# Three small reorderings in a TensorE-bound kernel: the attention's dense matmuls, V's job and the tail's products

## The chip, the cores and the metric

The kernel runs on one core of a Trainium2 chip. The metric is the device time of one execution in microseconds; the medians are over several executions. Every run named here is fast: the granted TensorE clock is 1.00 in all of them. Because the effects are of some tenths of a microsecond in 650, most of the argument is read from traces: each trace is one execution and has the start of its instructions (in four traces 52 matmul records are missing, see below), and the same wait in two traces agrees to about 0.01 us where nothing acts on it.

## The reference

The layer normalises x, computes attention in four segments of 512 tokens with a memory of the earlier segments, adds a token-mixing MLP, and adds x. The change touches the attention's second half only:

```python
for s in range(4):                                   # segments; 32 heads of 32
    logits = q_s k_s^T * scale + mask                # a causal mask
    a_dot  = softmax(logits) v_s
    a_mem  = phi(q_s) M / (phi(q_s) z + 1e-6)        # memory of earlier segments
    o      = g * a_mem + (1 - g) * a_dot             # g: a gate per head
    M, z   = M + phi(k_s)^T v_s, z + sum phi(k_s)
out = x + concat(o) @ wo + MLP(xn)                   # xn: x normalised
```

## The kernel before

The attention runs in 32 units, one for each segment and group of four heads. In a unit TensorE (PE) computes logits in two or three bursts, ScalarE (ACT) takes their exponentials (1.88 us each), GpSimd (POOL) masks the diagonal blocks of pT, and PE weighs the values in three parts for the unit before. Between these, PE runs *dense* jobs of eight 512-column matmuls: the projections q, k and V, and the output product ("wo"). How many dense matmuls stand between two steps is set by `cuts`. An even unit from 18 on reads: logits 0, `cuts[1]` dense matmuls, weighing part 0, `cuts[2]`, part 1, `cuts[3]`, part 2, logits 1, `cuts[5]`, logits 2, the rest.

```python
def unit_jobs(self, u):
    jobs = [self.wo_job(*self.wo_jobs.popleft())] if 10 <= u < self.QUOTA_FROM else []   # QUOTA_FROM is 18
    m = u // 4 + 1
    if m < 2 * N_SEG:
        jobs.append(self.v_job(m, u % 4))
    ...                                              # then q of unit u + 2, and k up to unit 15
# in attention()
    if u >= 18 and even:
        cuts = self.cut(total, (0, 4, 1, 4, 0, 9, 6))
```

Each job takes the next of two banks of PSUM (the memory that the matmuls of this kernel write their results to) in turn, so a job waits until the job *two before it* has been copied out of its bank. Who copies differs: q and (from unit 8) V are copied by ACT, k and wo by VectorE (DVE). wo's copy is an addition to `fin` of some 0.69 us.

```python
# q_job: ACT copies        # k_job: DVE copies        # v_job: ACT (for m > 2)        # wo_job: DVE adds to fin
def dense(self, n, side=True):
    while n > 0 and self.jobs:
        job = self.jobs[0]
        ...
        if b is None:
            b = job[1] = 6 + self.turn               # banks 6 and 7 in turn
            self.turn ^= 1
        ...                                          # matmuls up to the next stop
        if stop == 8:
            end(b)                                   # the copy, or the addition to fin
            self.jobs.popleft()
        elif self.side and stop in stops:
            self.side.popleft()()                    # one step of DVE's side work
```

Side work is DVE's part of the unit before and of the next: the scales, `pqT` (phi of q), `prod` (the weighed sums times their scales, 1.22 us), `o_s` (their addition), phi of k, and at times a normalisation (`xs`). DVE also fetches the weighed sums themselves ("the sums", `ost`, from banks 4 and 5; parts 0 and 2 of the weighing share bank 4). DVE carries these out in the order in which the program emits them.

The tail, after unit 31, multiplies the last segment's eight groups of oT (`o_s` transposed) with wo. Group 6 of oT comes by a DMA that transposes o_s of unit 30; group 7 by PE itself:

```python
...
product(3, 0, 6)                 # product n over groups 0 to 5
for n in range(3):
    product(n, 6, 7)             # the seventh group's part of products 0, 1, 2
product(4, 0, 7)
self.o_transpose(u, 4)
...
```

Of the kernel before, what the change touches and what calls it, by code (L numbers as in the profile page):

```python
# [386 lines left out]
class _Kernel:  # L387
# [1111 lines left out]
    def unit_jobs(self, u):  # L1499
        jobs = [self.wo_job(*self.wo_jobs.popleft())] if 10 <= u < self.QUOTA_FROM else []  # L1500
        m = u // 4 + 1
        if m < 2 * N_SEG:
            jobs.append(self.v_job(m, u % 4))
        if u + 2 < N_UNIT:
            jobs.append(self.q_job(u + 2))
            if u + 2 < N_UNIT // 2:
                jobs.append(self.k_job(u + 2))
            else:
                self.k_load(u + 2)
        if u >= self.QUOTA_FROM:  # L1510
            quota = self.QUOTA[u % 2] if u + 1 < N_UNIT else 100
            quota -= 8 * len(jobs) + sum(8 - j[0] for j in self.jobs)
            while quota > 0 and self.wo_jobs:
                jobs.append(self.wo_job(*self.wo_jobs.popleft()))
                quota -= 8
            self.left = max(-quota, 0)
        return jobs
# [5 lines left out]
    def attention(self):  # L1523
        self.jobs, self.turn, self.left = deque(), 0, 0
        self.side, self.stops = deque(), self.STOPS
        self.exps, self.in_etmp = [], [None] * 4
        self.wo_jobs = deque((c, half) for c in range(4 * (N_SEG - 1)) for half in range(2))
        self.jobs.extend([self.q_job(0), self.k_job(0)] + [self.v_job(0, c) for c in range(4)])
        self.dense(16)
        self.late_exps()  # L1530
        self.phi_k(0)
        self.k_transpose(0)
        self.jobs.extend([self.q_job(1), self.k_job(1)])
        self.dense(100)
        for u in range(N_UNIT):
            if u == N_GRP:
                t, R = _Walk(self.mem, self.B_AT + self.STG_AT, self.B_AT + self.S2_AT).take(
                    "oT2", [P, N_GRP, SEG_L], BF16, N_GRP)
                self.oT.append(t)
                self.R_oT.append(R)  # L1540
                self.load_fin(0)
                self.load_fin(1)
            if 1 <= u <= N_GRP:
                self.fw.dma(self.wo[:, u - 1, :], self.A_wo[(u - 1) * P:u * P, :], writes=[self.R_wo[u - 1]])
            even = u % 2 == 0
            self.jobs.extend(self.unit_jobs(u))
            total = 8 * len(self.jobs) - sum(j[0] for j in self.jobs) - self.left
            xn = self.XN_AT.index(u) + 4 if u in self.XN_AT else None
            if u in self.XN_AT[::4]:
                self.xn_load(xn)  # L1550
                self.xn_load(xn + 1)
            if u >= 18 and even:
                cuts = self.cut(total, (0, 4, 1, 4, 0, 9, 6))
            elif u < 10 or u >= 14 and total <= 26:
                cuts = self.cut(total, (0, 4, 2, 4, 1, 13, 8) if even else (7, 3, 2, 4, 1, 15))
            else:
                cuts = self.cut(total, (0, 4, 2, 2, 2, 14, 8) if even else (7, 3, 2, 2, 2, 16))
            end = u >= N_UNIT - 4
            self.stops = self.STOPS_FEW if total <= 26 and u >= 14 else self.STOPS
            self.dense(cuts[0])  # L1560
            self.logits(u, 0)
            self.dense(cuts[1], end)
            while end and self.side:
                self.side.popleft()()
            if u:
                self.weigh(u - 1, 0)
            self.dense(cuts[2], False)
            if u:
                self.weigh(u - 1, 1)
            self.dense(cuts[3], False)  # L1570
            if u:
                self.weigh(u - 1, 2)
                steps = self.combine(u - 1)
                last = steps[-1]
                steps[-1] = lambda u=u, last=last: (last(), self.o_transpose_dma(u - 1))
                self.side.append(steps.pop(0))
            if N_GRP <= u:
                self.side.append(lambda u=u: self.phi_q(u))
            if u:
                self.side.extend(steps)  # L1580
            if u + 1 < N_UNIT:
                self.side.append(lambda u=u: (self.phi_k(u + 1), self.k_transpose(u + 1)))
            if xn is not None:
                self.side.append(lambda c=xn: (self.xn_scale(c), self.xn_transpose(c), c % 4 < 2 and self.xn_load(c + 2)))
            self.dense(cuts[4])
            self.logits(u, 1)
            if even:
                self.dense(cuts[5])
                self.logits(u, 2)
            self.dense(8 * len(self.jobs) - sum(j[0] for j in self.jobs) - self.left)  # L1590
        while self.side:
            self.side.popleft()()
        self.tail()
# [10 lines left out]
    def tail(self):  # L1604
        fw = self.fw
        s, u = N_SEG - 1, N_UNIT - 1
        fin, R_fin = self.fin, self.R_fin
        for i in range(2, 4):
            self.load_fin(4 * s + i)
        fw.wait_outputs(3)  # L1610

        def product(n, j0, j1, cols=((0, 512),)):
            i, h, b = n // 2, n % 2, (6 + self.turn, 0, 1, 2, 3, 7 - self.turn, 5, 4)[n]
            for p, (c0, c1) in enumerate(cols):
                with fw.group(reads=self.R_wo[j0:j1] + self.R_oT[s % 3][j0:j1], writes=[self.R_bank[b]]):
                    for jc in range(j0, j1):
                        fw.mm(self.ps[:, b, c0:c1], self.oT[s % 3][:, jc, i * P:(i + 1) * P],
                              self.wo[:, jc, h * 512 + c0:h * 512 + c1], start=(jc == 0), stop=(jc == N_GRP - 1))
                if j1 < N_GRP:
                    return  # L1620
                dst = fin[i][:, h * 512 + c0:h * 512 + c1]
                R = Res("fin")
                R.w = R_fin[i][h].w
                fw.op("dve", lambda e: e.tensor_tensor(dst, self.ps[:, b, c0:c1], dst.bitcast(F16), op=ALU.add),
                      reads=[self.R_bank[b], R], writes=[R])
                fw.dma(self.out_d[:, 4 * s + i, h * 512 + c0:h * 512 + c1], dst, reads=[R],
                       is_output=True, issuer=("sp", "act")[p % 2])
                b = (b + 1) % 3

        product(0, 0, 6)  # L1630
        product(1, 0, 6)
        self.weigh(u, 0)
        self.weigh(u, 1)
        product(2, 0, 6)
        self.weigh(u, 2)
        for step in self.combine(u):
            step()
        product(3, 0, 6)
        for n in range(3):
            product(n, 6, 7)  # L1640
        product(4, 0, 7)
        self.o_transpose(u, 4)
        product(3, 6, 7)
        product(5, 0, 5)
        for n in range(5):
            product(n, 7, 8)
        product(5, 5, 8)
        product(6, 0, 8)
        product(7, 0, 8, ((0, 256), (256, 384), (384, 512)))
# [28 lines left out]
```

## Time and profile before

| what | value |
|---|---|
| median time | 653.07 us (652.82 to 653.62, 6 runs) |
| span of the profiled execution | 651.30 us |
| from its start to the first logits | 387.46 us |
| first to last logits ("attention") | 243.48 us |
| last logits to the last matmul ("tail") | 17.86 us |

Lines from the profile page of the kernel before: the span, the busy time of each engine with its share of the span, and the chain of work that ended last, by engine.

```profile
span 651.3 us, 11181 instructions
...
PE 645.6 (99%) x4611; PEld 303.2 (47%) x4611; DVE 433.7 (67%) x808; ACT 281.3 (43%) x305; POOL 153.0 (23%) x179
...
PE 94%; DVE 2%; DMA 1%; ACT 1%; POOL 1%; issue 0%; DVEq 0%
```

PE is busy 99% of the span and makes 94% of the chain. The change adds and removes no matmul, so it can win only PE's waits. The view of waits of the kernel before, for PE, has five lines (who waited for whom: us in total, times, longest). These two lie in the stretch that the change touches; two others (DVE's brow, 1.3 us, and h, 0.3) lie ahead of the attention, and one (ACT's pT, 0.2) is in unit 0:

```profile
PE ps_all L199 <- DMA oT<-o_s: 0.5, 1, 0.5
PE ps_all L199 <- POOL pT L1368: 0.4, 2, 0.2
```

These figures are too small, and a learner should see why. A 512-column matmul stands in the trace with 0.38 us, but the next one starts 0.216 us after it. The Trainium skill ("Perfetto Trace Analysis", "Tensor Engine Instruction") says that a TensorE instruction's end is estimated and not observed. A wait shorter than the 0.16 us between these two figures is therefore invisible, and a longer one shows only its rest. So I read *starts*: for each matmul I took the start of the next, less 0.216 us after 512 columns, 0.056 after 132, 0.025 after 33; in front of a logits burst 0.096 us are regular, and behind one 0.09 to 0.10, and these are taken off too. What remains is called *excess*. The largest in the kernel before:

| where (unit) | excess, us | what PE waited for |
|---|---|---|
| tail | 0.70 | the DMA that transposes o_s of unit 30 |
| weighing, units 20, 22, 24 | 0.37, 0.22, 0.37 | POOL's mask |
| weighing, unit 16 | 0.25 | POOL's mask |
| V's job, unit 11 | 0.30 | DVE's copy of k out of the bank |
| V's job, units 22 and 26 | 0.16, 0.07 | ACT's copy of the job two before |
| logits 1, unit 0 | 0.22 | the exponentials before; the same in every run |
| logits 0, even units from 20 | 0.09 each | the exponentials before |

The following fences are from the timelines of the kernel before (start in us, length in us, engine, line, operation, output and inputs, forms, count; in brackets the engine's idle time and who ended it). First the tail:

```profile
635.64 2.03 SPq L221 DMA_TRANSPOSE oT<-o_s  x1
...
637.95 1.46 PE L199 MATMUL ps_all<-wo,oT 128*128 128x512 bf16 x6
...
639.94 2.33 PE L199 MATMUL ps_all<-wo,oT 128*128 128x512 bf16 x10 [0.53 <-DMA oT<-o_s]
...
642.11 0.39 PE L205 MATMUL ps_all<-ident,o_s 128*128 128x128 bf16 x4
```

The DMA is issued at 635.64. PE's six matmuls from 637.95 are through by 639.25 (6 times 0.216), but the next starts at 639.94: 0.70 us, of which the bracket shows 0.53. Next unit 20, where the fourth line is weighing part 0:

```profile
545.66 1.22 DVE L1465 TENSOR_TENSOR prod<-ost,srec 128x1024 bf16<-128x1024 bf16 x1
...
545.86 2.28 POOL L1368 TENSOR_SCALAR_AFFINE_SELECT pT<-pT 128x512 bf16<-128x512 bf16 x2 [2.78 <-ACT pT L1364]
...
546.27 1.04 PE L199 MATMUL ps_all<-wo,oT 128*128 128x512 bf16 x4
...
547.52 0.25 PE L199 MATMUL ps_all<-vA,pT 128*128 128x33 bf16 x4 [0.21 <-POOL pT L1368]
```

POOL's two masks start 0.2 us after DVE's `prod`. Taken singly, the first mask lasts 1.51 us here, against a usual 0.63; PE has done its four matmuls by 547.15 and starts weighing at 547.52. Further on, at the border of units 20 and 21, the job after the logits is V's, and its bank was q's:

```profile
554.77 0.59 ACT L1253 ACTIVATE qT<-ps_all 128x512 bf16<-128x512 f32 x1
...
555.14 0.40 PE L199 MATMUL ps_all<-qT,kT 32*128 32x512 bf16 x4
...
555.50 0.59 PE L199 MATMUL ps_all<-wv,xnT 128*128 128x512 bf16 x2
```

ACT's copy of q ends at 555.36, V starts at 555.50, only 0.04 us later than it would without. Then unit 11, where PE waits for the copy of k:

```profile
472.16 1.00 DVE L1230 SCALAR_TENSOR_TENSOR mtmp<-kT,mtmp 128x512 bf16<-128x512 bf16 x1
...
473.09 0.68 DVE L1262 CAST kT<-ps_all 128x512 bf16<-128x512 f32 x1
...
473.30 0.39 PE L199 MATMUL ps_all<-wo,oT 128*128 128x512 bf16 x1
...
473.82 0.60 PE L199 MATMUL ps_all<-wv,xnT 128*128 128x512 bf16 x2
```

The copy ends at 473.77 and V starts at 473.82 instead of 473.52. Last, weighing part 2 of unit 12, before which nothing waits:

```profile
482.37 0.68 DVE L1262 CAST kT<-ps_all 128x512 bf16<-128x512 f32 x1
...
482.97 1.23 DVE L1418 TENSOR_TENSOR ost<-ps_all,eps 128x396 bf16<-128x396 f32 x2
...
483.86 0.56 PE L199 MATMUL ps_all<-vA,pT 128*128 128x33 bf16 x16
484.11 0.68 DVE L1307 TENSOR_TENSOR fin<-ps_all,fin 128x512 bf16<-128x512 f32 x1
```

Two sums run from 482.97 to 484.20; part 2 needs the bank of the first one and starts at 483.86. `fin` follows at 484.11, where DVE would otherwise be waiting for PE.

### The profile page before, as it was taken

The page shows a single profiled execution, that of the slowest core. Times are in us where ns is not written, and L with a number is a line of the kernel's source. Part 1 is how long each engine was busy: PE and PEld are TensorE (multiplying, and loading weights), DVE is VectorE, ACT ScalarE, POOL GpSimd, SP SyncE. Part 2 cuts the span into 40 slices and gives each one's busy share as a digit, 9 for nine tenths or more (in the row PEclk, how much of TensorE's full clock was granted, in tenths as well). Part 3 has the DMA queues.
Part 4 walks back from the last instruction along what each step waited for, and adds up shares of the span by engine and source line. Part 5 has one row for each costly group of instructions (what it writes and reads, how often), then busy time and mean ns, then how long its engine had stood idle before and what let it go on. Part 6 is the DMA issues. An engine that isn't in the chain of part 4 may idle for free.

```text
span 651.3 us, 11181 instructions
## 1 busy us (share of the span) xinstructions
PE 645.6 (99%) x4611; PEld 303.2 (47%) x4611; DVE 433.7 (67%) x808; ACT 281.3 (43%) x305; POOL 153.0 (23%) x179
## 2 busy tenths in 40 slices
PE   8999999999999999999999999999999999999998
PEld 3444444444444444444444444444545444445444
DVE  6975675665655663744738326767888977777895
ACT  6543232232210000111101047778867788879760
POOL 2510000000011220120201203434333445554450
DMA  9804233242498937628263946979654685435425
GB/s 298 220 0 130 65 109 85 65 119 75 129 257 214 237 101 210 165 94 235 82 200 110 260 128 167 188 180 218 131 129 102 159 171 130 113 93 128 113 83 139
DMA packets 190123, 95.00 MB, mean 146 GB/s; under 512 B 108664, under 2 KB 176248, under 8 KB 190072
## 3 DMA queue, kind: packets, MB, share of 16 engines
q1 hardware_dynamic: 189928, 94.25, 56.8%
q8 instruction: 36, 0.59, 0.4%
q14 instruction: 15, 0.12, 0.1%
q10 hardware_dynamic: 144, 0.03, 0.0%
HBM read 69.23 MB, written 11.53 MB: 124 GB/s over the span
## 4 chain that ended last, share of the span: by engine, by line
PE 94%; DVE 2%; DMA 1%; ACT 1%; POOL 1%; issue 0%; DVEq 0%
PE ps_all L199 94%; ACT pT L1364 1%; DMA oT<-o_s 1%; DVE ln_st L587 1%; POOL pT L1368 0%; DMA xin<-in_A_x_dram 0%; DVE h L627 0%; POOL ln_rs L611 0%; DVE mtmp L1230 0%; DVE mtmp L1228 0%; DVE prod L1465 0%; DVE pqT L1230 0%; DVE fin L1307 0%; DVE ln_mv L590 0%; DVE kT L1262 0%
## 5 line engine op out<-in xcount | busy, mean ns | idle before, releaser
L1364 ACT ACTIVATE pT<-ps_all 128x2048 bf16<-128x2048 f32 x80 | 150.2, 1877 | 46.8 <-PE ps_all L199 46.3
L1368 POOL TENSOR_SCALAR_AFFINE_SELECT pT<-pT 128x512 bf16<-128x512 bf16 x128 | 104.5, 834 | 161.9 <-ACT pT L1364 161.7
L689 DVE TENSOR_TENSOR part<-ps_all,part 128x512 f32<-128x512 f32 x84 | 57.7, 690 | 109.3 <-PE ps_all L199 88.6
L1075 POOL TENSOR_TENSOR part<-part,stg 128x512 f32<-128x512 f32 x24 | 33.0, 1402 | 284.7 <-DVE part L689 267.7
L199 PE MATMUL ps_all<-wv,xnT 128*128 128x512 bf16 x256 | 68.5, 380 | 0.2
L746 ACT ACTIVATE g<-part,b1c 128x512 f16<-128x512 f32 x36 | 26.0, 722 | 98.7 <-DVE part L689 98.7
L199 PE MATMUL ps_all<-xnT,wq 128*128 128x512 bf16 x256 | 66.2, 380 | 0.0
L199 PE MATMUL ps_all<-wo,oT 128*128 128x512 bf16 (+2 forms) x272 | 63.6, 367 | 0.5 <-DMA oT<-o_s 0.5
L694 ACT ACTIVATE part<-ps_all 128x512 f32<-128x512 f32 x24 | 14.0, 596 | 101.4 <-PE ps_all L199 67.1
L199 PEld LDWEIGHTS ps_all<-vA,pT 128*128 128x128 bf16 x1280 | 45.7, 96 | 20.6 <-DVE prod L1465 1.9
L1418 DVE TENSOR_TENSOR ost<-ps_all,eps 128x396 bf16<-128x396 f32 (+1 forms) x72 | 37.0, 522 | 24.3 <-PE ps_all L199 23.7
L199 PE MATMUL ps_all<-g,w2s 128*128 128x512 f16 x224 | 51.0, 379 | 0.0
L199 PE MATMUL ps_all<-g,sum 128*128 128x512 f16 x224 | 51.0, 379 | 0.0
L199 PE MATMUL ps_all<-gT,sum 128*128 128x512 f16 x224 | 50.3, 379 | 0.0
L199 PE MATMUL ps_all<-vA,pT 128*128 128x33 bf16 x1280 | 48.5, 177 | 0.6 <-POOL pT L1368 0.4
L199 PE MATMUL ps_all<-h,sum 128*128 128x512 f16 x192 | 45.2, 379 | 0.0
L199 PE MATMUL ps_all<-h,w1s 128*128 128x512 f16 x192 | 44.9, 379 | 0.0
L199 PE MATMUL ps_all<-hT,sum 128*128 128x512 f16 x192 | 43.6, 379 | 0.0
L199 PEld LDWEIGHTS ps_all<-wo,oT 128*128 128x128 bf16 x272 | 24.0, 98 | 27.3 <-issue 4.2
L199 PEld LDWEIGHTS ps_all<-g,w2s 128*128 128x128 bf16 x224 | 21.9, 98 | 26.4
L199 PEld LDWEIGHTS ps_all<-g,sum 128*128 128x128 f16 x224 | 21.9, 98 | 26.4 <-DVE part L689 0.2
L199 PEld LDWEIGHTS ps_all<-gT,sum 128*128 128x128 f16 x224 | 21.9, 98 | 26.5 <-DVE gT L663 0.3
(118 smaller groups left out, 874.4 us busy)
## 6 DMA issues: line engine op xcount, KB each, us to landing
w2s<-in_B_w_dram SPq DMA_DIRECT2D x8, 1792.0 KB, 9.5
w1s<-in_B_w_dram SPq DMA_DIRECT2D x12, 1024.0 KB, 5.5
wq<-in_A_wq_dram SPq DMA_DIRECT2D x32, 256.0 KB, 3.2
xs<-in_A_x_dram SPq DMA_DIRECT2D x24, 256.0 KB, 3.4
stg<-in_A_x_dram SPq DMA_DIRECT2D x16, 256.0 KB, 2.9
out_dram<-stg SPq DMA_DIRECT2D x16, 256.0 KB, 3.5
wk<-in_A_wk_dram SPq DMA_DIRECT2D x16, 256.0 KB, 3.4
fin<-out_dram SPq DMA_DIRECT2D x16, 256.0 KB, 3.2
```

Source lines behind the costliest of these rows:

```text
L199: ins = self.nc.tensor.matmul(*args, **kwargs)
L587: fw.op("dve", lambda e: e.bn_stats(st[:, 6 * h:6 * h + 6], src[:, 512 * h:512 * h + 512]), reads=[self.R_xin[c]], writes=[R])
L689: self.fw.op("dve", lambda e: e.tensor_tensor(self.tmp[dst][:], self.bank(b), self.tmp[src][:], op=ALU.add), reads=[self.R_bank[b], self.R ...
L694: self.fw.op("act", lambda e: e.activation(self.tmp[dst][:], self.bank(b), ACT.Copy), reads=[self.R_bank[b]], writes=[self.R_tmp[dst]])
L746: self.fw.op("act", lambda e: e.activation(self.gB[f % 2][half][:, f // 2, :], src, ACT.Gelu_apprx_tanh, bias=self.b1c[:, f:f + 1], scale= ...
L1075: fw.op("pool", lambda e: e.tensor_tensor(self.tmp[t][:], self.tmp[t][:], self.stg[k][:, 512 * half:512 * half + 512], op=ALU.add), reads= ...
L1364: fw.op("act", lambda e: e.activation(dst, src, ACT.Exp, scale=SCALE), reads=self.R_bank[0:4], writes=[R[v % 2][kb] for v, kb, _ in blocks ...
L1368: fw.op("pool", lambda e: e.affine_select(d, d, pattern=[[0, 4], [1, P]], compare_op=ALU.is_ge, fill=0.0, base=0, channel_multiplier=-1), ...
L1418: fw.op("dve", lambda e: e.tensor_tensor(dst, src, eps, op=ALU.add), reads=[self.R_bank[b], self.R_eps], writes=[self.R_ost[o][part]])
```

## The change

Its intent is to put work in front of three of these waits. The diff, whole:

```diff
-            jobs.append(self.v_job(m, u % 4))
+            jobs.insert(0, self.v_job(m, u % 4))
...
             if u >= 18 and even:
-                cuts = self.cut(total, (0, 4, 1, 4, 0, 9, 6))
+                cuts = self.cut(total, (0, 5, 1, 4, 0, 9, 5))
...
         product(3, 0, 6)
-        for n in range(3):
+        product(4, 0, 6)
+        for n in (0, 1, 2, 4):
             product(n, 6, 7)
-        product(4, 0, 7)
```

The first part matters in units 10 to 17 only, where wo's job came ahead of V's. The second puts a fifth dense matmul ahead of weighing part 0 in the seven even units from 18, and takes it from behind logits 2. The third puts six matmuls of product 4 ahead of the first that needs the DMA's result.

## The prediction

> **What bounds the kernel.** TensorE. The page has PE busy 645.6 of 651.3 us, and 94% of the chain of waits is matmuls; the granted clock is 1.00. No matmul is added or removed, so only PE's waits can be won. The waits view shows few (a DMA 0.5 us, POOL 0.4, ACT 0.2), but a matmul's modelled end hides short ones, so I took starts from the timeline: 512-column matmuls follow each other every 0.216 us, which agrees with the Trainium skill (TensorE: Matmul & The Clock Gate, "Wait — 56ns, not 53.3ns?": 215.7 ns). What exceeds that, beside a regular 0.1 to 0.17 us around every logits burst, is: in the tail 0.70 us (639.03 to 639.94, waiting for the DMA transpose of the seventh group's oT, issued at 635.64); before the weighing in units 20, 22, 24: 0.37, 0.22, 0.37; in unit 16: 0.25 (POOL's mask); in unit 11: 0.30 (V's bank waits for DVE's copy of kT, which ends at 473.77). The rest is under 0.17 each. So at most some 2 us can be won.
>
> **Step 1, tail.** Six matmuls (1.30 us) move ahead of the matmul that waits for the transpose. The wait (0.70) is covered with 0.6 to spare. The o_s transposes behind it then start at about 641.4; o_s is ready at 640.91. Everything up to the last store moves. -0.70 us.
>
> **Step 2, one more dense matmul ahead of the weighing, even units from 18.** Counting the cuts: 0,4,1,4,0,9,6 becomes 0,5,1,4,0,9,5 in seven units. POOL's first mask, 1.52 us instead of the usual 0.63 because it starts while DVE multiplies prod (545.66 to 546.88), is what PE waits for; the Trainium skill (SBUF — State Buffer, "SBUF: two separate sides") tells of an exclusive port pair, and this agrees. 0.216 is covered in each of units 20, 22, 24. But the matmul is taken from behind the third logits. There the next logits come 0.27 us after the exp's end and would come 0.06 after it, the shortest distance seen elsewhere: free. In units 20 and 24, however, V's job that follows takes the bank of q, whose ACT copy ends (555.36, 585.54) just before V's start (555.50, 585.65), so that 0.2 comes back as a wait for ACT. Only unit 22 keeps it; units 18, 26, 28, 30 had no wait. -0.2 us.
>
> **Step 3, V first in units 10 to 17.** V's copy is on ACT, the output product's add (fin, 0.69 us) on DVE. Before, fin ran mostly where DVE was idle, ahead of the third sums; now it falls into DVE's densest stretch. Gains: in unit 10 one side step fewer goes ahead of the copy of kT, so unit 11's 0.30 vanishes; in unit 15 fin delays prod, POOL goes first, and unit 16's 0.25 vanishes. Losses: in units 11 and 13 DVE has no idle time from fin to the next sums, so these come 0.65 us later, and the third weighing of units 12 and 14, which takes their bank, should wait some 0.3 to 0.4 each (slack now about 0.3); possibly 0.1 to 0.2 in units 15 to 18. Net about 0, anywhere from -0.5 to +1.
>
> **Sum.** -0.9 us: 652.2 us. Range 651.2 to 653.4. Faster by over 2%: 0.005, within 2%: 0.99, slower: 0.005.
>
> **What would show it.** Right: no wait for the DMA transpose in the tail; the waits before the weighing at 0.15, 0, 0.15 in units 20, 22, 24; new ACT waits of 0.2 at V in units 21 and 25; no DVE wait in unit 11; new DVE waits ahead of the third weighing in units 12 and 14. Wrong: the sums' lateness absorbed by DVE idle time or shorter POOL conflicts (651.2); or the DVE backlog growing because POOL's masks lock it further (over 653).

## The result, and the profile after

| what | before | after |
|---|---|---|
| median time, us | 653.07 (6 runs) | 652.32 (652.14 to 652.74, 6 runs) |
| span of the profiled execution | 651.30 | 650.55 |
| start to first logits | 387.46 | 387.50 |
| attention | 243.48 | 243.40 |
| tail | 17.86 | 17.15 |

The ratio is 0.9988, with a 95% interval of 0.9976 to 1.0001. A ratio is the mean time of one kernel's fast runs over that of the other's of the same rounds, so it is not quite the ratio of the medians that I quote. The interval includes 1: by it the change cannot be told from none, although all six runs after (at most 652.74) lie below all six before (at least 652.82). What each part does is therefore read from the traces. The same three lines of the page, and PE's waits, of the changed kernel:

```profile
span 650.5 us, 11182 instructions
...
PE 645.9 (99%) x4611; PEld 303.6 (47%) x4611; DVE 433.7 (67%) x808; ACT 281.4 (43%) x305; POOL 154.2 (24%) x179
...
PE 94%; DVE 3%; ACT 2%; issue 1%; DMA 0%; POOL 0%; DVEq 0%
```

```profile
PE ps_all L199 <- DVE ost L1418: 0.3, 2, 0.2
PE ps_all L199 <- ACT qT L1253: 0.2, 1, 0.2
```

The waits for the DMA and for POOL have left the list. Two new ones are in it: for the sums (`ost`) on DVE, and for ACT's copy of q. The tail of the changed kernel, from its timeline:

```profile
635.60 2.77 SPq L221 DMA_TRANSPOSE oT<-o_s  x1
...
637.91 3.61 PE L199 MATMUL ps_all<-wo,oT 128*128 128x512 bf16 x16
...
641.36 0.39 PE L205 MATMUL ps_all<-ident,o_s 128*128 128x128 bf16 x4
```

Sixteen matmuls run without a break from 637.91; the transposes behind them start 0.75 us earlier than before, of which 0.04 was already won. Units 20 and 21 of the changed kernel:

```profile
545.88 1.22 DVE L1465 TENSOR_TENSOR prod<-ost,srec 128x1024 bf16<-128x1024 bf16 x1
...
546.09 2.28 POOL L1368 TENSOR_SCALAR_AFFINE_SELECT pT<-pT 128x512 bf16<-128x512 bf16 x2 [2.77 <-ACT pT L1364]
...
546.50 1.04 PE L199 MATMUL ps_all<-wo,oT 128*128 128x512 bf16 x4
...
547.74 0.25 PE L199 MATMUL ps_all<-vA,pT 128*128 128x33 bf16 x4
```

```profile
554.99 0.59 ACT L1253 ACTIVATE qT<-ps_all 128x512 bf16<-128x512 f32 x1
...
555.15 0.39 PE L199 MATMUL ps_all<-qT,kT 32*128 32x512 bf16 x4
...
555.73 0.59 PE L199 MATMUL ps_all<-wv,xnT 128*128 128x512 bf16 x2 [0.18 <-ACT qT L1253]
```

The fifth dense matmul lies ahead of the weighing, whose excess is now 0.15 us. The distance from POOL's start to the weighing is 1.65 us as before (545.86 to 547.52): the mask sets it. The logits at 555.15 come 0.22 us sooner after the exponentials than before, and V's excess has grown from 0.04 to 0.25 us: it starts 0.15 us after the end of ACT's copy (555.58), where before it was 0.14 (555.36 to 555.50). What was won at the weighing is given back at V. Units 11 and 12 of the changed kernel:

```profile
472.17 0.68 DVE L1262 CAST kT<-ps_all 128x512 bf16<-128x512 f32 x1
...
473.57 0.59 PE L199 MATMUL ps_all<-wo,oT 128*128 128x512 bf16 x2
```

```profile
482.70 0.68 DVE L1262 CAST kT<-ps_all 128x512 bf16<-128x512 f32 x1
...
483.30 1.03 DVE L1418 TENSOR_TENSOR ost<-ps_all,eps 128x396 bf16<-128x396 f32 x2
...
483.91 0.57 PE L199 MATMUL ps_all<-vA,pT 128*128 128x33 bf16 x16 [0.16 <-DVE ost L1418]
```

In unit 11 k's copy now goes ahead of phi of k (`mtmp`), ends at 472.85 and nobody waits. In unit 12 the copy of k comes later in respect to PE, the sums with it, and weighing part 2 waits 0.32 us for them. Unit 14 is alike (0.33 us).

### The profile page after: what moved, and what is told of

Same layout as the page of the kernel before. It is cut to its first block, busy times and chain, and to the rows that moved or that the text cites. A ratio compares the mean times of both kernels' runs of the same rounds, so it can differ in the third digit from the quotient of the medians.

```text
span 650.5 us, 11182 instructions
## 1 busy us (share of the span) xinstructions
PE 645.9 (99%) x4611; PEld 303.6 (47%) x4611; DVE 433.7 (67%) x808; ACT 281.4 (43%) x305; POOL 154.2 (24%) x179
## 4 chain that ended last, share of the span: by engine, by line
PE 94%; DVE 3%; ACT 2%; issue 1%; DMA 0%; POOL 0%; DVEq 0%
PE ps_all L199 94%; ACT pT L1364 1%; DVE prod L1465 1%; DVE ln_st L587 1%; DMA xin<-in_A_x_dram 0%; DVE h L627 0%; DVE ost L1418 0%; POOL ln_rs L611 0%; DVE mtmp L1230 0%; DVE kT L1262 0%; DVE fin L1307 0%; DVE mtmp L1228 0%; ACT qT L1253 0%; ACT vA L1293 0%; DVE ln_mv L590 0%
## 5 line engine op out<-in xcount | busy, mean ns | idle before, releaser
L199 PEld LDWEIGHTS ps_all<-xnT,wq 128*128 128x128 bf16 x256 | 22.6, 97 | 25.4 <-issue 5.3
```

Of the source, the lines that this page charges most:

```text
L199: ins = self.nc.tensor.matmul(*args, **kwargs)
```

## The experiments

All lists of excess below are made as described above. "Attention" and "tail" are the two stretches of the table; I compare these and not the whole span, because the start to the first logits differs by up to 0.5 us between profiled executions (387.37 to 387.89) although no experiment but e8 and e10, which reorder PE's checks in the whole program, touches it.

| run | edit | median, us | ratio (95% interval) | attention, us | tail, us |
|---|---|---|---|---|---|
| before | | 653.07 | | 243.48 | 17.86 |
| after | all three parts | 652.32 | 0.9988 (0.9976 to 1.0001) | 243.40 | 17.15 |
| e1 | tail | 652.39 | 0.9985 (0.9972 to 0.9997) | 243.48 | 17.15 |
| e2 | V first | 653.72 | 1.0004 (0.9991 to 1.0016) | 243.68 | 17.96 |
| e3 | cuts | 652.91 | 0.9994 (0.9980 to 1.0007) | 243.20 | 17.87 |
| e4 | tail, cuts, q by DVE | 651.95 | 0.9978 (0.9965 to 0.9990) | 243.02 | 17.15 |
| e5 | V first in 11, 13 | 654.05 | 1.0010 (0.9998 to 1.0023) | 244.17 | 18.19 |
| e6 | a selection | 651.76 | 0.9976 (0.9963 to 0.9989) | 242.78 | 17.15 |
| e7 | e6, q by DVE | 651.61 | 0.9974 (0.9960 to 0.9987) | 242.54 | 17.15 |
| e8 | e7, order of waits | 651.17 | 0.9968 (0.9955 to 0.9980) | 242.37 | 17.15 |
| e9 | product in halves | 653.20 | 1.0000 (0.9987 to 1.0012) | 243.09 | 17.94 |
| e10 | e8 and e9 | 651.03 | 0.9966 (0.9952 to 0.9980) | 242.10 | 17.15 |

The runs of the kernel before had medians of 653.47 us beside e1 to e4, 653.43 beside e5 to e8 and 653.19 beside e9 and e10. The intervals of the change, e2, e3, e5 and e9 include 1; what is said of these rests on one profiled execution each, though the waits of the change recur in e2, e3 and e5. The traces of e5 to e8 lack 52 matmul records each, 47 of them in the attention and 3 in the tail. The other starts are not affected, but a missing 512-column matmul looks like an excess of 0.216 us; these places are left out of the lists, and e5's wait in the tail is not counted, because a record is missing beside it.

### e1: the tail alone

```diff
         product(3, 0, 6)
-        for n in range(3):
+        product(4, 0, 6)
+        for n in (0, 1, 2, 4):
             product(n, 6, 7)
-        product(4, 0, 7)
```

> The tail alone. My theory: the 0.70 us wait for the DMA transpose of the seventh group's oT vanishes and nothing else changes: profiled span 651.3 - 0.70 = 650.6 us, time ratio 0.9989. Rival (the three parts only work together, or the last stores set the end): span stays within 0.2 us of 651.3, with a wait of like size further down the tail.

The tail went from 17.86 to 17.15 us and the attention stayed at 243.48 with every excess in its place. The tail's wait was 0.70, 0.80, 0.72 and 0.78 us in the four complete traces that have the old tail (before, e2, e3, e9) and absent in all that have the new one, where the tail takes 17.15 us each time. My theory holds; the rival is out.

### e2: V first alone

```diff
-            jobs.append(self.v_job(m, u % 4))
+            jobs.insert(0 if u in range(10, 18) else len(jobs), self.v_job(m, u % 4))
```

> V first in units 10 to 17 alone. My theory, with sizes as in the changed kernel's trace: -0.30 (unit 11's wait for the copy of kT), +0.32 and +0.33 (third weighing of units 12 and 14 waits for the sums on DVE), +0.05, and in unit 16 -0.25 +0.09: net +0.2 us, span 651.5, ratio 1.0004. Rival (it was put in because it pays): span 650.8 or less, the new DVE waits absent without the other two parts.

The attention grew by 0.20 us. The excess in unit 11 (0.30) went; 0.32 and 0.33 came in units 12 and 14 for the sums, 0.05 in unit 15 for fin; in unit 16 0.25 for POOL became 0.09 for the sums. The sum agrees, so V first as a whole does not pay. In time it cannot be told from nothing (1.0004).

### e3: the extra dense matmul alone

```diff
-                cuts = self.cut(total, (0, 4, 1, 4, 0, 9, 6))
+                cuts = self.cut(total, (0, 5, 1, 4, 0, 9, 5))
```

> One more matmul ahead of the weighing alone. My theory: waits for POOL ahead of the weighing shrink by 0.22 each in units 20, 22, 24 (0.37, 0.22, 0.37 to 0.16, 0, 0.16), but V in units 21 and 25 waits 0.25 and 0.16 longer for ACT's copy of q; net -0.3 us, span 651.0, ratio 0.9995. Rival (the matmul is simply moved under a wait, seven units gain): span 650.6 or less, and no longer waits at V.

The attention fell by 0.28 us. The excess ahead of the weighing is 0.16, none, 0.16 us in units 20, 22, 24; V's is 0.25 and 0.16 in units 21 and 25. The parts also add up: e2's +0.20 and e3's -0.28 make -0.08, and the changed kernel's attention is 0.08 us shorter than before's. In time e3 cannot be told from nothing either (0.9994).

### e4: is it ACT's copy that gives the matmul back?

```diff
     (on top of the tail and the cuts; in q_job's end)
+            if u in (22, 26):
+                fw.op("dve", lambda e: e.tensor_copy(self.qT[k][:], self.bank(b)), ...)
+            else:
                 fw.op("act", lambda e: e.activation(self.qT[k][:], self.bank(b), ACT.Copy), ...)
```

> Tail and cuts, with q of units 22 and 26 copied from its bank by DVE in place of ACT. My theory: V's waits in units 21 and 25 are for ACT's copy, which queues behind the exp, so they fall to the regular 0.17; gain -0.70 -0.3 and a further -0.25 and -0.16: span 649.9, ratio 0.9978, unless DVE's copy (0.69 us) comes late or delays the next sums. Rival (V waits in truth for the exp itself or for logits' order): the waits in units 21 and 25 stay at 0.42 and 0.33, span 650.3.

From the timeline of e4 at the border of units 20 and 21:

```profile
554.73 0.68 DVE L1254 CAST qT<-ps_all 128x512 bf16<-128x512 f32 x1
...
555.17 0.39 PE L199 MATMUL ps_all<-qT,kT 32*128 32x512 bf16 x4
...
555.55 0.59 PE L199 MATMUL ps_all<-wv,xnT 128*128 128x512 bf16 x2
```

DVE's copy ends at 555.41, before ACT would have ended. V's excess fell from 0.25 to 0.05 us in unit 21 and from 0.16 to none in unit 25: ACT's copy, queued behind an exponential, was the cause. The gain was not whole: the logits 2 of units 22 and 26 now show an excess of 0.09 us each. They start 0.14 us after the exponentials' end instead of 0.06. e8 looks into that.

### e5: do the sums come late because fin left its hole?

```diff
+            jobs.insert(0 if u in (11, 13) else len(jobs), self.v_job(m, u % 4))
```

> V first in units 11 and 13 alone, no other part. My theory (fin leaves a hole in DVE's work and pushes everything up to the next sums): the third weighing of units 12 and 14 waits 0.32 each for the sums, and unit 11's wait of 0.30 for the copy of kT stays, since unit 10's side steps are untouched: span 651.3 + 0.65 = 651.95, ratio 1.0010. Rival (these waits come from V's copy on ACT, or from the eight units' order together): the two waits are absent or under 0.1 and the span within 0.2 of 651.3.

The attention grew by 0.69 us: 0.32 in unit 12 and 0.33 in unit 14 for the sums, and unit 11's wait stayed at 0.31. From e5's timeline in unit 12:

```profile
483.85 1.04 DVE L1418 TENSOR_TENSOR ost<-ps_all,eps 128x396 bf16<-128x396 f32 x2
...
484.47 0.58 PE L199 MATMUL ps_all<-vA,pT 128*128 128x33 bf16 x16 [0.16 <-DVE ost L1418]
```

Two units' order is enough for both waits, and unit 10's order has no part in them. The two programs' instructions for DVE, laid side by side, show the cause. A line marked - stands there in the kernel before, + in e5, and unmarked lines in both; this is the stretch of unit 11:

```
 L1262 TensorCopy kT_3217<-ps_all 128x512
+L1418 TensorTensor ost_3257<-ps_all,eps 128x396 x2
+L1418 TensorTensor ost_3257<-ps_all,eps 128x264
+L1429 TensorTensor MZ_3321<-MZ_3321,ps_all 128x132
+L1431 TensorTensor MZbf<-MZ_3321,diag 128x132
 L1307 TensorTensor fin_3332<-ps_all,fin_3332 128x512
-L1418 TensorTensor ost_3257<-ps_all,eps 128x396 x2
-L1418 TensorTensor ost_3257<-ps_all,eps 128x264
-L1429 TensorTensor MZ_3321<-MZ_3321,ps_all 128x132
-L1431 TensorTensor MZbf<-MZ_3321,diag 128x132
 L1461 Reciprocal srec<-ost_3257 128x32
```

`fin`, which DVE carried out ahead of the sums while it would have waited for PE, now comes behind them, and so ahead of everything up to unit 12's sums. These come later by it, and with them weighing part 2 of unit 12. The traces bear it out: from the end of L1431 to the start of unit 12's sums it is 5.21 us in the kernel before (477.76 to 482.97) and 5.81 in e5 (478.04 to 483.85), 0.60 more, about the 0.68 that `fin` takes, and DVE is never idle for more than 0.04 us in between. Two other lengths change there and cancel: `prod` takes 1.66 instead of 1.22 us, and the first step of phi of k 0.28 instead of 0.72.

### e6: only what pays

```diff
     (on top of the tail)
+            jobs.insert(0 if u in (10, 15) else len(jobs), self.v_job(m, u % 4))
+                cuts = self.cut(total, (0, 5, 1, 4, 0, 9, 5) if u in (22,) else (0, 4, 1, 4, 0, 9, 6))
```

> Only what pays: the tail, V first in units 10 and 15 alone, one more matmul ahead of the weighing in unit 22 alone. My theory: -0.70 (tail), -0.30 (unit 11's wait), -0.16 (unit 16: 0.25 for POOL becomes 0.09 for the sums), -0.22 (unit 22), no DVE waits in units 12 and 14, no longer ACT waits in 21 and 25: span 649.9, ratio 0.9979. Rival (the parts need each other): no better than the whole change, 650.5.

The attention is 242.78 us, 0.70 below the kernel before (0.30, 0.20 and 0.21 of it at units 11, 15 to 16 and 22), and the tail has its 0.71. V first in two of eight units, and the extra matmul in one of seven, do better than all of them: the other places cost or give back what they win. The time is 0.9976 of before's.

### e7 and e8: q by DVE again, and the order of two semaphore checks

```diff
     (e7: e6 with the cuts in units 20, 22 and 24, and e4's copy; e8: e7 and)
-        for t in need.values():
+        order = sorted(need.values(), key=lambda t: isinstance(t.key, tuple)) if es.name == "pe" else need.values()
+        for t in order:
             es.wait_tok(t)
```

> As e6, with the extra matmul in units 20, 22 and 24 and DVE copying q of units 22 and 26. My theory: a further -0.43 at the weighings, less two waits of 0.09 at the third logits of units 22 and 26 that e4 showed: span 649.7, ratio 0.9975. Rival (e6's V order and e4's DVE copy get in each other's way on DVE): 650 or more.

> As e7, and PE's waits of one group asked for in another order (engine semaphores ahead of DMA semaphores). In the kernel before, logits that wait for ACT with a second semaphore checked after it start 0.14 us after the exp's end, those with ACT checked last 0.06. If the order is the cause, the 0.09 waits at the logits of even units from 20 and at the third logits of units 22 and 26 vanish; part of it comes back as waits for POOL or ACT behind them: span 649.4 (0.2 to 0.4 below e7). Rival (the 0.14 comes from the ACT queue or the first use of the operands): no change, 649.7.

e7's attention is 0.24 us below e6's (I expected about 0.25), and its logits 2 of units 22 and 26 wait 0.09 us as in e4. In e8 all of these 0.09 waits are gone, with those ahead of logits 0 in even units. The logits 0 of unit 20 in e7 and then in e8, from their timelines:

```profile
543.51 1.88 ACT L1368 ACTIVATE pT<-ps_all 128x2048 bf16<-128x2048 f32 x1 [1.04 <-PE ps_all L199]
...
545.53 0.40 PE L199 MATMUL ps_all<-qT,kT 32*128 32x512 bf16 x4
```

```profile
543.42 1.88 ACT L1369 ACTIVATE pT<-ps_all 128x2048 bf16<-128x2048 f32 x1 [1.05 <-PE ps_all L200]
...
545.35 0.40 PE L200 MATMUL ps_all<-qT,kT 32*128 32x512 bf16 x4
```

The exponential ends at 545.39 and the logits start 0.14 us later in e7; at 545.30 and 0.05 later in e8. The two traces show what differs: in e7, as in the kernel before, a separate semaphore instruction waits for ACT, and after it the weight load checks a second semaphore, that of a DMA which landed long before (at 540.34 in e7); in e8 the weight load itself waits for ACT, and the other check is over by then. Part of the gain came back behind it, as expected: 0.25 instead of 0.16 for POOL in units 20 and 24, and 0.16 instead of 0.07 for ACT in units 26 and 30; some waits of 0.06 to 0.09 us are new in units 10, 22 and 28. The net is 0.17 us of attention.

### e9 and e10: is it one DVE instruction that holds POOL off?

```diff
-            fw.op("dve", lambda e: e.tensor_tensor(self.prod[:], ...[P, 32, D_HEAD]..., op=ALU.mult), ...)
+            parts = ((0, 16), (16, 32)) if u in (18, 20, 22) else ((0, 32),)
+            for a0, a1 in parts:
+                fw.op("dve", lambda e: e.tensor_tensor(self.prod[:, a0:a1], ..., op=ALU.mult), ...)
     (e9: on the kernel before; e10: on e8)
```

> The kernel before, with the product of units 18, 20 and 22 (done by DVE in units 19, 21, 23) cut into two instructions of half the size; nothing else. My theory: POOL's first mask takes 1.51 us because one DVE instruction of 1.22 us holds it off to its end, so with two of some 0.6 the mask gets in between and ends 0.6 earlier; the waits of 0.37, 0.22, 0.37 ahead of the weighing in units 20, 22, 24 vanish without a matmul being moved: span 651.3 - 0.96 = 650.3, ratio 0.9985. Rival (DVE's work as a whole slows POOL in that stretch, or POOL waits for something else): the mask stays over 1.3 us and the waits stay, span 651.3.

From e9's timeline in unit 20:

```profile
546.09 1.72 DVE L1467 TENSOR_TENSOR prod<-ost,srec 128x512 bf16<-128x512 bf16 x2
...
546.30 2.01 POOL L1368 TENSOR_SCALAR_AFFINE_SELECT pT<-pT 128x512 bf16<-128x512 bf16 x2 [2.78 <-ACT pT L1364]
...
547.58 0.26 PE L199 MATMUL ps_all<-vA,pT 128*128 128x33 bf16 x4
...
549.10 1.03 DVE L1418 TENSOR_TENSOR ost<-ps_all,eps 128x396 bf16<-128x396 f32 x2
...
549.71 0.57 PE L199 MATMUL ps_all<-vA,pT 128*128 128x33 bf16 x16
```

Half of this came true. POOL's first mask, taken singly, lasts 0.97 us instead of 1.51, and no excess is left ahead of the weighing in units 20, 22 and 24 (0.96 us won). But the second half of `prod` now waits for POOL (1.00 us instead of some 0.6), all that DVE does behind it comes later, and weighing part 2 of units 20 and 24 waits 0.28 us each for the sums. The attention fell by 0.39 us, not 0.96. In the median time even that is not to be seen: the profiled run lost 0.43 us of it ahead of the first logits and 0.08 in the tail's DMA wait, and the interval of the ratio, 0.9987 to 1.0012, doesn't tell 0.4 us from none. So the expected total failed, while what holds POOL off is shown.

> As e8, with the products of units 18, 20 and 22 cut in two. My theory: the waits of 0.25, 0.09 and 0.25 for POOL that e8 still has ahead of the weighing in units 20, 22, 24 vanish; since the logits there come 0.09 sooner, part may come back as a wait for ACT: span 649.4 - 0.5 = 648.9, ratio 0.9960. Rival: no gain over e8 (span 649.4), because the time comes back at the third logits or at V.

e10's attention is 0.27 us below e8's; POOL's waits went and 0.15 us for the sums came in units 20 and 24, which I had not thought of in this place. Its ratio, 0.9966, and e8's, 0.9968, cannot be told apart. Both intervals lie below 1, so both are faster than the kernel before. No run put them beside the change, and its interval overlaps theirs; but their medians (651.17 and 651.03) lie below all six of its times, and in the traces its attention is 1.03 and 1.30 us longer than theirs.

## Why the prediction was right

The measured median, 652.32 us, lies 0.12 us from the predicted 652.2. That closeness is in part luck: the six runs of each kernel spread over 0.6 to 0.8 us, and the misses of the terms below have both signs. The stated range, 651.2 to 653.4, even holds the time before, 653.07, so it says little; what was tested is the list of waits, and all that it names came.

| term | predicted, us | measured, us | run |
|---|---|---|---|
| tail | -0.70 | -0.71 | e1 |
| extra dense matmul | -0.2 | -0.28 | e3 |
| V first | about 0, from -0.5 to +1 | +0.20 | e2 |
| sum | -0.9 | -0.75 | medians; the same in the spans |

- *The tail.* Right in mechanism and size; six matmuls (1.30 us) more than cover the DMA. This part is nearly all of the gain: 0.71 of 0.75 us; the other two make 0.08 in the attention, and the start to the first logits took back 0.04.
- *The extra matmul.* Right: in the seven units it moves, only unit 22 keeps the whole 0.216 us. The expected excesses (0.15, 0, 0.15; V 0.2 in units 21 and 25) were measured at 0.15, none, 0.15, and 0.25, 0.16. I left out what unit 18's excess of 0.04 and V's slack in unit 25 add, which makes most of the 0.08. e4 shows that it is ACT's copy that gives the rest back.
- *V first.* Right in all its waits: unit 11's 0.30 vanished, part 2 of units 12 and 14 waits 0.32 and 0.33 (predicted 0.3 to 0.4), unit 16's wait for POOL went. I gave the net as about 0 although my own terms summed to somewhat over it, and it is +0.20; this is the largest miss of the sum.
- *Why POOL's mask is long.* The Trainium skill ("SBUF — State Buffer", "SBUF: two separate sides") says that the pair of ports that DVE and GpSimd share is an exclusive lock: between a DVE operation with two SBUF inputs, as `prod` is, and a GpSimd operation that reads SBUF, as the mask does, whichever starts first has the pair for the whole instruction. The traces agree: the mask takes 1.51 us behind a whole `prod` and 0.97 behind half of one, and in unit 15 of the changed kernel, where the mask comes first, it takes 0.97 and `prod` 1.66 instead of 1.22.

What stays open: why the start to the first logits differs by up to 0.5 us between executions, and why e9's time shows none of its 0.39 us. No run was made for either.

## What to carry to other kernels

When an engine is busy 99% of the time, list its waits one by one from the starts of its instructions, and for each piece of work that a change moves look at both ends: the place it covers and the place it leaves. In unit 20 a dense matmul taken from behind an exponential cost as much at the next bank as it won; an addition moved out of DVE's idle time in one unit came back as a wait of 0.32 us in the next. Apply such a reordering only in the units where the trace shows the wait: V first in two units of eight and the extra matmul in one of seven won 0.70 us of attention, where all of them together won 0.08.

## What the Trainium skill lacked or had wrong

- "SBUF — State Buffer" tells that the loser of the shared port pair blocks fully, and the runs agree. It states its rule, that issue order decides who blocks ("Who interferes with whom"), for a pair of operations, and doesn't work out the case in which GpSimd waits behind one DVE instruction and DVE has the following one ready. Here the order of issue held: in unit 15 of the changed kernel POOL's mask, whose record starts at 515.46 while `pqT` runs, went ahead of `prod`, whose record starts at 515.85 and which then took 1.66 us instead of 1.22; with `prod` in halves POOL got in between them and the second half took 1.00 us. The cost changes sides and doesn't vanish.
- I found on no page what a second, already satisfied semaphore check costs a PE instruction behind the one that it really waits for: logits started 0.14 us after the exponential's end so, and 0.05 to 0.06 with the late semaphore checked last (e7, e8).
- "Perfetto Trace Analysis" tells that a matmul's end is estimated; it doesn't say what follows for reading waits. Here a 512-column matmul stands with 0.38 us and the next starts after 0.216, so a wait up to 0.16 us is not seen as idle time and one of 0.70 is shown as 0.53.
